# Two staging buffers for decoded weight blocks, one early block, second products three units behind

## The chip, the cores and the metric

The kernel runs on one core of a Trainium2 chip. The time is the device time of one execution, in microseconds, of that core. TensorE is called PE here, VectorE DVE, ScalarE ACT, GpSimd POOL; SP issues the DMA transfers.

## The reference

Three layers follow each other, all in float32.

```python
mask = q_assign[:, :, :, None] == k_assign[:, :, None, :]   # nearest of 16 centroids per head
scores = np.where(mask, scale * q @ k.T, -1e9)              # 2 x 8 heads, 768 tokens, 64 wide
attn = softmax(scores)
x = (attn @ v)                                              # becomes 1536 tokens x 512
h = x @ w_in;  g = np.maximum(0.01 * h, h); x = g @ w_out   # first MLP, 512 -> 2048 -> 512
h = x @ w_in2; r = np.maximum(h, 0); x = (r * r) @ w_out2   # second MLP, same sizes
```

The weights arrive as 64-bit floats; the kernel turns them into float32 itself.

## The kernel before

**Precision.** A float32 matrix is carried as two parts, a rounded one and the remainder (`xh` and `xl`, `wh` and `wl`, `gh` and `gl`), and a product is three matmuls: high by high, high by low, low by high.

**Attention** takes 48 steps of two row tiles. In a step PE makes scores `S`, DVE their row maxima `nm`, ACT the exponentials `e`, POOL divides them by their sums, PE transposes them (`T`, 12 transposes in three groups of four), ACT rounds each group to `eh`, DVE subtracts to `el`, and PE multiplies by the values (`A`, 12 matmuls). ACT and DVE then fold `A` into `xt` (lines 461 and 470). `A` has one PSUM buffer, so the next step's `A` waits for that fold. At the end of a head pair POOL makes `xh` and `xl` from `xt`.

**The MLPs.** A weight block is 128 of the 2048 hidden columns, `w_in` and `w_out` together, 16 blocks for each MLP, 32 in all. A unit is one block by one of three token blocks of 512, 96 units. For each unit `g1` (line 725) makes `h` with 12 matmuls, `act` makes `g` and its two parts on ACT and DVE, and `g2` (line 767) adds 12 matmuls into four sums `o`. `g2` of a unit is written `LAG` units behind its `g1`. Units go by groups of 2, 2, 4, 4 and so on blocks; in a group, token block by token block, the group's blocks in turn. After a group the four sums are added to `acc` (`flush`). There are four PSUM buffers for `h` and four for `o`.

**Weight blocks.** `decode_pieces` gives six pieces for a block: load (1 MB, a DMA by SP), `mag` on ACT (line 128), `shift`, `low` and `sign` on DVE (lines 132, 138, 145), and `split`, which makes `wh` on ACT (line 156) and `wl` on POOL (line 157). The raw block and its float32 form, `wraw` and `wt`, stand in a staging pool of one buffer each, taken from `stg[-1]`, the pool opened last. There are two such pools one after the other: `stg`, opened for the last head pair, and `stgb`, opened after attention. The first `EARLY` blocks are decoded beside the last head pair, through `stg`; the others use `stgb`, whose memory was that of exponentials `e` in attention. Eight blocks of finished weights are kept: those whose number modulo 8 is under 4 in the pool `wpx`, the others in `wpb`.

**The order.** Until six steps before the end of attention every engine's order is written out by hand (`PLAN`). From there the Tile scheduler puts the instructions in an order by its own estimate of times, once, when the program is built; each engine then runs its own list strictly in that order. The loads of SP are in program order throughout. Names such as `h_3740` carry a number that the build gives to each buffer; the same work has other numbers in the two kernels.

Of the kernel before, what the change touches and what calls it, by code (L numbers as in the profile page):

```python
# [10 lines left out]
I32 = mybir.dt.int32  # L11
# [41 lines left out]
def attention_moe_moe_kernel(  # L53
# [14 lines left out]
    NT, DM = out.shape  # L68
# [7 lines left out]
    NBLK = NT // N  # L76
    G = 4
    GROUPS = ([2, 2] + [G] * (NF // G - 1), [G] * (NF // G))
    EARLY = 2
    RING = 8  # L80
    WARM = (9,4,10)

# [29 lines left out]
    stg = []  # L112

    def decode_pieces(ci):

        m, f = divmod(ci, NF)
        st = {}

        def load():
            st["raw"] = stg[-1].tile([128, 2 * DM, 2], I32, tag="wraw", name="wraw")  # L120
            nc.sync.dma_start(
                out=st["raw"].rearrange("p a b -> p (a b)"), in_=(w1, w2)[m][f].bitcast(I32)
            )

        def mag():
            t = stg[-1].tile([128, 2 * DM], I32, tag="wt", name="wt")
            st["t"] = t
            nc.scalar.mul(out=t.bitcast(F32), in_=st["raw"][:, :, 1].bitcast(F32), mul=W_SHIFT)

        def shift():  # L130
            t = st["t"]
            nc.vector.tensor_scalar(
                out=t, in0=t, scalar1=3, scalar2=None, op0=ALU.logical_shift_left
            )

        def low():
            t = st["t"]
            nc.vector.scalar_tensor_tensor(  # L138
                out=t, in0=st["raw"][:, :, 0], scalar=29, in1=t,
                op0=ALU.logical_shift_right, op1=ALU.bitwise_or,  # L140
            )

        def sign():
            t = st["t"]
            nc.vector.scalar_tensor_tensor(
                out=t, in0=st["raw"][:, :, 1], scalar=-0x80000000, in1=t,
                op0=ALU.bitwise_and, op1=ALU.bitwise_or,
            )

        def split():  # L150
            t = st["t"].bitcast(F32)
            pool = next(q for q, n in ring if ci % RING < n)
            wh = pool.tile([128, 2 * DM], F32R, tag="wh", name="wh")
            wl = pool.tile([128, 2 * DM], F32R, tag="wl", name="wl")
            weights[m, f] = (wh, wl)
            nc.scalar.copy(out=wh, in_=t)  # L156
            nc.gpsimd.tensor_tensor(out=wl, in0=t, in1=wh.bitcast(F32), op=ALU.subtract)  # L157

        return [load, mag, shift, low, sign, split]

    def pool_copy(out, in_):
# [510 lines left out]
    }  # L672

    early = [f for i in range(EARLY) for f in decode_pieces(i)]
    for u in range(-1, NU + 5):
        if u == NU - UPP:
# [7 lines left out]
        for op in PLAN[FIRST[u] if p == 0 else u % UPP].split():  # L684
            if ":" in op:
                name, lag = op.split(":")
# [5 lines left out]
            else:  # L692
                name, ahead = op.split("@")
# [13 lines left out]
    ast.close()  # L707


    gp = ctx.enter_context(tc.tile_pool(name="gp", bufs=3, reuse_waits="tile"))  # L710
    ring.append((ctx.enter_context(tc.tile_pool(name="wpb", bufs=RING - G, reuse_waits="tile")), RING))
    stg.append(ctx.enter_context(tc.tile_pool(name="stgb", bufs=1, reuse_waits="tile")))
    accp = ctx.enter_context(tc.tile_pool(name="accp", bufs=1, reuse_waits="tile"))
# [37 lines left out]
    def g2(m, b, f, g, first, last, gh, gl):  # L751
        wh, wl = weights[m, f]
        for o in range(4):
            if first:
                outs[o] = ps_o.tile([128, N], F32, tag="o", name="o")
            if m == 0:
                ws = slice(DM + o * 128, DM + (o + 1) * 128)
                mm = ((wh[:, ws], gh), (wh[:, ws], gl), (wl[:, ws], gh))
            else:
                ts = slice(o * 128, (o + 1) * 128)  # L760
                mm = (
                    (gh[:, ts], wh[:, DM:]),
                    (gh[:, ts], wl[:, DM:]),
                    (gl[:, ts], wh[:, DM:]),
                )
            for i, (l, r) in enumerate(mm):
                nc.tensor.matmul(  # L767
                    out=outs[o],
                    lhsT=l,
                    rhs=r,  # L770
                    start=(first and i == 0),
                    stop=(last and i == 2),
                )
            if last:
                flush(m, b, g, o, outs[o])
# [25 lines left out]
    for m in range(2):  # L801
        f = 0
        for g, size in enumerate(GROUPS[m]):
            for i in range(size):
                if ci >= EARLY:
                    pcs = decode_pieces(ci)
                    at = last + i * (began - last) // size
                    n = max((began - last) // size, 1)
                    for k, pc in enumerate(pcs):
                        plan.setdefault(at + k * n // len(pcs), []).append(pc)  # L810
                ci += 1
            last = began
            for b in range(NBLK):
                for i in range(size):
                    units.append((m, b, f + i, g, i == 0, i == size - 1))
            began = len(units)
            f += size
    LAG = 2
    pend = []
    for U in range(len(units) + LAG):  # L820
        if U < len(units):
            m, b, f = units[U][:3]
            pend.append((*units[U], *act(m, g1(m, b, f))))
            for pc in plan.get(U, []):
                pc()
        if U == len(units) + LAG - 1:
            with tc.manual_schedule(engines={mybir.EngineType.PE}):
                g2(*pend.pop(0))
        elif U >= LAG:
            g2(*pend.pop(0))  # L830
# [47 lines left out]
```

## Time and profile before

| | us |
|---|---|
| median of 3 runs | 793.64 (792.76 to 794.53) |
| the profiled execution | 790.98 |
| its span, first to last instruction | 789.2 |
| PE busy in the span | 771.2 |

The sums of the prediction are made against the profiled execution. It lies 2.66 us under the median of the runs, and 1.78 us of it lie outside the span. Attention fills roughly the first 245 us of the span, the MLPs the rest, with some 20 us in which both are at work. Rows of the timeline give the start in us from the span's beginning, the duration, the engine, the line and the instruction; in brackets stands the idle time before it and what ended it. A matmul's duration there overlaps that of the next one, so the pace of matmuls is read from start to start. In the lines of the order, and of the profile, `S`, `T`, `A`, `h` and `o` are the PSUM tiles named above.

### The profile page before, as it was taken

To read this page: it belongs to the slowest core of one execution; us is meant where nothing else is said; L and a number is where in the kernel's file an instruction comes from. 1 tells how busy PE (TensorE), PEld (TensorE's weight loads), DVE (VectorE), ACT (ScalarE), POOL (GpSimd) and SP (SyncE) were. 2 spreads that over 40 slices of the span, in tenths; PEclk is the share of its full clock that TensorE was granted. 3 is DMA by queue.
4 is the path that set the end of the run, shared out by engine and by line. 5 is a ranking of instruction groups with operands and counts; after the bars stand their busy time and mean duration, and the time that the engine had idled before them with its cause. 6 is when DMAs were issued, how large, how long until landed. Compare 5 with 4: busy or idle time off the path is not lost.

```text
span 789.2 us, 11011 instructions
## 1 busy us (share of the span) xinstructions
PE 771.2 (98%) x4147; PEld 664.4 (84%) x4147; DVE 538.0 (68%) x772; ACT 412.7 (52%) x759; POOL 292.0 (37%) x257
## 2 busy tenths in 40 slices
PE   8999999999989999999999999999999999999998
PEld 8899999999977778888888888888888888888886
DVE  5899999999997378876665568387356547533333
ACT  6988988988996464443432344345344334222221
POOL 2989889888854322122220124352022012100000
PEclk9999999999999999999999999999999999999999
DMA  7584574564510323123221022013112103000102
GB/s 222 120 205 108 109 173 116 113 153 91 125 54 2 107 106 107 60 100 108 107 107 54 1 106 82 26 54 108 54 53 107 54 0 108 1 0 1 45 23 94
DMA packets 16005, 66.35 MB, mean 84 GB/s; under 512 B 2704, under 2 KB 2704, under 8 KB 10960
## 3 DMA queue, kind: packets, MB, share of 16 engines
q1 hardware_dynamic: 15952, 65.64, 28.7%
q8 instruction: 33, 0.54, 0.3%
q14 instruction: 20, 0.16, 0.1%
HBM read 44.60 MB, written 3.15 MB: 60 GB/s over the span
## 4 chain that ended last, share of the span: by engine, by line
PE 81%; DVE 11%; ACT 4%; DMA 1%; issue 1%; POOL 1%; SPq 0%; DVEq 0%; ACTq 0%
PE o L767 33%; PE h L725 33%; PE A L448 5%; PE T L413 5%; PE S L350 5%; DVE el L430 3%; DVE nm L373 3%; ACT e L383 2%; DVE xt L470 1%; ACT eh L424 1%; DVE ds L276 1%; PE ohT L305 1%; DVE m L275 1%; DMA rqk<-qk 1%; DVE wt L138 1%
## 5 line engine op out<-in xcount | busy, mean ns | idle before, releaser
L157 POOL TENSOR_TENSOR wl<-wt,wh 128x1024 fp32r<-128x1024 f32 x32 | 76.8, 2400 | 292.6 <-ACT wh L156 235.6
L725 PE MATMUL h<-xh,wh 128*128 128x512 f32 x384 | 150.6, 393 | 2.2 <-DVE g L739 2.2
L725 PE MATMUL h<-xh,wl 128*128 128x512 f32 x384 | 150.6, 392 | 0.0
L725 PE MATMUL h<-xl,wh 128*128 128x512 f32 x384 | 150.5, 392 | 0.0
L746 DVE TENSOR_TENSOR gl<-g,gh 128x512 fp32r<-128x512 f32 x96 | 95.4, 994 | 47.6 <-ACT gh L745 47.5
L430 DVE TENSOR_TENSOR el<-T,eh 128x512 fp32r<-128x512 f32 x144 | 94.8, 683 | 7.8 <-ACT eh L424 6.0
L745 ACT CAST gh<-g 128x512 fp32r<-128x512 f32 x96 | 59.6, 621 | 73.0 <-DVE g L742 42.7
L400 POOL TENSOR_SCALAR e<-e,r 128x768 f32<-128x768 f32 x96 | 88.0, 927 | 20.1 <-DVE r L397 14.7
L373 DVE TENSOR_REDUCE nm<-S 128x1 f32<-128x768 f32 x96 | 90.7, 946 | 4.6 <-PE S L254 2.2
L350 PE MATMUL S<-hb 128*128 128x384 f32 (+1 forms) x384 | 90.6, 350 | 3.0 <-ACT e L383 2.6
L383 ACT ACTIVATE e<-S,nm 128x768 f32<-128x768 f32 x96 | 87.0, 906 | 11.7 <-DVE nm L373 7.4
L742 DVE TENSOR_TENSOR g<-t 128x512 f32<-128x512 f32 x48 | 39.4, 822 | 72.8 <-ACT t L741 72.7
L725 PEld LDWEIGHTS h<-xh,wh 128*128 128x128 f32 x384 | 72.2, 188 | 18.5 <-DVE g L739 2.6
L741 ACT ACTIVATE t<-h 128x512 f32<-128x512 f32 x48 | 28.7, 598 | 112.0 <-PE h L725 111.9
L424 ACT CAST eh<-T 128x512 fp32r<-128x512 f32 x144 | 79.6, 585 | 12.9 <-PE T L413 12.3
L725 PEld LDWEIGHTS h<-xh,wl 128*128 128x128 f32 x384 | 72.2, 188 | 16.0
L725 PEld LDWEIGHTS h<-xl,wh 128*128 128x128 f32 x384 | 72.2, 188 | 15.9
L448 PE MATMUL A<-eh,vv 128*128 128x256 f32 x288 | 79.5, 306 | 3.5 <-DVE xt L470 3.5
L413 PE MATMUL T<-ident,e 128*128 128x128 f32 x576 | 81.0, 274 | 1.1 <-DVE el L430 1.0
L738 ACT ACTIVATE t<-h 128x512 f32<-128x512 f32 x48 | 28.6, 598 | 95.6 <-PE h L725 95.6
L767 PE MATMUL o<-gh,wl 128*128 128x512 f32 x192 | 75.3, 392 | 0.0
L767 PE MATMUL o<-gh,wh 128*128 128x512 f32 x192 | 74.5, 393 | 0.8 <-DVE xt L470 0.8
(105 smaller groups left out, 1454.0 us busy)
## 6 DMA issues: line engine op xcount, KB each, us to landing
wraw<-w SPq DMA_DIRECT2D x32, 1024.0 KB, 4.7
hb<-spl SPq DMA_DIRECT2D x14, 576.0 KB, 4.8
hb<-spl SPq DMA_DIRECT2D x42, 192.0 KB, 5.0
rqk<-qk SPq DMA_DIRECT2D x16, 384.0 KB, 4.5
rv<-v SPq DMA_DIRECT2D x8, 384.0 KB, 3.6
out<-ob SPq DMA_DIRECT2D x12, 256.0 KB, 2.1
twice<-qk SPq DMA_DIRECT2D x8, 192.0 KB, 6.4
hb<-st SPq DMA_DIRECT2D x28, 48.0 KB, 2.7
```

The costliest lines, as they stand in the source:

```text
L157: nc.gpsimd.tensor_tensor(out=wl, in0=t, in1=wh.bitcast(F32), op=ALU.subtract)
L350: nc.tensor.matmul(out=s[:, c, 0:HALF], lhsT=hb[0:k, a, i * 128 : (i + 1) * 128], rhs=hb[0:k, b, c * HALF : (c + 1) * HALF], start=(a == 0 ...
L373: nc.vector.tensor_reduce(out=n, in_=s_t[t][:, :, 0:HALF], axis=AX.XY, op=ALU.max, negate=True)
L383: nc.scalar.activation(out=e.rearrange("p (a b) -> p a b", a=2), in_=s_t.pop(t)[:, :, 0:HALF], func=AF.Exp, bias=n_t.pop(t), scale=1.0, ac ...
L400: nc.gpsimd.tensor_scalar(out=e_t[t], in0=e_t[t], scalar1=r_t[t // 2][:, t % 2 : t % 2 + 1], scalar2=1.0, op0=ALU.mult, op1=ALU.mult,)
L413: nc.tensor.transpose(T[:, o : o + 128], e_t[2 * u + b][:, kc * 128 : (kc + 1) * 128], ident)
L424: nc.scalar.copy(out=eh[:, 2 * g : 2 * g + 2, :].rearrange("p a b -> p (a b)"), in_=T_t[u, g])
L430: nc.vector.tensor_tensor(out=el[:, 2 * g : 2 * g + 2, :].rearrange("p a b -> p (a b)"), in0=T_t.pop((u, g)), in1=eh[:, 2 * g : 2 * g + 2, ...
L448: nc.tensor.matmul(out=A, lhsT=w, rhs=m[:, kc, :], start=(kc == 0 and i == 0), stop=(kc == KC - 1 and i == 1),)
L725: nc.tensor.matmul(out=h, lhsT=w[:, ws], rhs=x[:, kk, c], start=(kk == 0 and i == 0), stop=(kk == HP - 1 and i == 2),)
L746: nc.vector.tensor_tensor(out=gl, in0=g, in1=gh.bitcast(F32), op=ALU.subtract)
L767: nc.tensor.matmul(out=outs[o], lhsT=l, rhs=r, start=(first and i == 0), stop=(last and i == 2),)
```

## The change

Blocks from number `EARLY` on take the two staging pools in turns, even blocks `stg` and odd ones `stgb`; the early block uses `stg`. `EARLY` goes from 2 to 1, so block 1 is no longer decoded beside attention. `LAG` goes from 2 to 3, and `gh` and `gl` have four buffers in place of three, which moves `wpb` and `stgb` up by 4 KB in each partition.

```diff
--- before.py
+++ after.py
@@ -76,7 +76,7 @@
     NBLK = NT // N
     G = 4
     GROUPS = ([2, 2] + [G] * (NF // G - 1), [G] * (NF // G))
-    EARLY = 2
+    EARLY = 1
     RING = 8
     WARM = (9,4,10)
 
@@ -115,15 +115,16 @@
 
         m, f = divmod(ci, NF)
         st = {}
+        own = ci % 2 if ci >= EARLY else 0
 
         def load():
-            st["raw"] = stg[-1].tile([128, 2 * DM, 2], I32, tag="wraw", name="wraw")
+            st["raw"] = stg[own].tile([128, 2 * DM, 2], I32, tag="wraw", name="wraw")
             nc.sync.dma_start(
                 out=st["raw"].rearrange("p a b -> p (a b)"), in_=(w1, w2)[m][f].bitcast(I32)
             )
 
         def mag():
-            t = stg[-1].tile([128, 2 * DM], I32, tag="wt", name="wt")
+            t = stg[own].tile([128, 2 * DM], I32, tag="wt", name="wt")
             st["t"] = t
             nc.scalar.mul(out=t.bitcast(F32), in_=st["raw"][:, :, 1].bitcast(F32), mul=W_SHIFT)
 
@@ -707,7 +708,7 @@
     ast.close()
 
 
-    gp = ctx.enter_context(tc.tile_pool(name="gp", bufs=3, reuse_waits="tile"))
+    gp = ctx.enter_context(tc.tile_pool(name="gp", bufs=4, reuse_waits="tile"))
     ring.append((ctx.enter_context(tc.tile_pool(name="wpb", bufs=RING - G, reuse_waits="tile")), RING))
     stg.append(ctx.enter_context(tc.tile_pool(name="stgb", bufs=1, reuse_waits="tile")))
     accp = ctx.enter_context(tc.tile_pool(name="accp", bufs=1, reuse_waits="tile"))
@@ -815,7 +816,7 @@
                     units.append((m, b, f + i, g, i == 0, i == size - 1))
             began = len(units)
             f += size
-    LAG = 2
+    LAG = 3
     pend = []
     for U in range(len(units) + LAG):
         if U < len(units):
```

The first place is DVE beside the last steps of attention, from the row that takes the maxima of `S`. Before:

```order
L373 TENSOR_REDUCE nm_3447<-S_3412 128x1
L132 TENSOR_SCALAR wt_3493<-wt_3493 128x1024
L470 TENSOR_TENSOR xt_3091<-A_3372,xt_3091 64x256
L397 RECIPROCAL r_3368<-r_3368 128x2
L430 TENSOR_TENSOR el_3379<-T_3418,eh_3378 128x512
L138 SCALAR_TENSOR_TENSOR wt_3493<-wraw_3491,wt_3493 128x1024
L430 TENSOR_TENSOR el_3445<-T_3428,eh_3444 128x512
L373 TENSOR_REDUCE nm_3474<-S_3450 128x1
L430 TENSOR_TENSOR el_3445<-T_3455,eh_3444 128x512
L145 SCALAR_TENSOR_TENSOR wt_3493<-wraw_3491,wt_3493 128x1024
L397 RECIPROCAL r_3434<-r_3434 128x2
L470 TENSOR_TENSOR xt_3484<-A_3438,xt_3484 64x256
```

and now:

```order
L374 TENSOR_REDUCE nm_3406<-S_3382 128x1
L471 TENSOR_TENSOR xt_3091<-A_3370,xt_3091 64x256
L398 RECIPROCAL r_3366<-r_3366 128x2
L374 TENSOR_REDUCE nm_3441<-S_3410 128x1
L431 TENSOR_TENSOR el_3377<-T_3416,eh_3376 128x512
L431 TENSOR_TENSOR el_3439<-T_3422,eh_3438 128x512
L431 TENSOR_TENSOR el_3439<-T_3449,eh_3438 128x512
L374 TENSOR_REDUCE nm_3468<-S_3444 128x1
L471 TENSOR_TENSOR xt_3478<-A_3432,xt_3478 64x256
L398 RECIPROCAL r_3428<-r_3428 128x2
```

The three DVE pieces of block 1 (`wt_3493`) are gone from between attention's rows; the fold of `A` (`xt`) stands next to the maxima.

The second place is PE at the end of attention's matmuls, around the first unit's second product. Before, from the row ahead of the last `A` matmul, `wh_3609` being block 1 and `wh_3424` block 0:

```order
L448 MATMUL A_3693<-eh_3666,vv_3072 128x256
L448 MATMUL A_3693<-el_3667,vv_3072 128x256
L725 MATMUL h_3910<-xl_62,wh_3609 128x512
L725 MATMUL h_3910<-xh_61,wl_3610 128x512
L767 MATMUL o_3814<-gh_3757,wh_3424 128x512
L767 MATMUL o_3814<-gl_3758,wh_3424 128x512
L767 MATMUL o_3814<-gh_3757,wl_3425 128x512
L767 MATMUL o_3818<-gh_3757,wh_3424 128x512
L767 MATMUL o_3818<-gl_3758,wh_3424 128x512
```

and now, from the end of the first unit's second product on, `wh_3757` being block 1 and `wh_3598` block 0:

```order
L768 MATMUL o_3851<-gh_3746,wh_3598 128x512
L768 MATMUL o_3851<-gl_3747,wh_3598 128x512
L768 MATMUL o_3851<-gh_3746,wl_3599 128x512
L726 MATMUL h_3765<-xh_61,wh_3757 128x512
L726 MATMUL h_3765<-xl_62,wh_3757 128x512
L726 MATMUL h_3788<-xh_61,wh_3598 128x512
L726 MATMUL h_3788<-xl_62,wh_3598 128x512
L726 MATMUL h_3788<-xh_61,wl_3599 128x512
```

Before, six units' `h` (the first two whole) were spread among the last `T` and `A`; now only the first unit's 12 matmuls stand there, the rest of attention's matmuls follow in one piece, and after the 12 matmuls of the first unit's second product the next on the list reads block 1. Two matmuls of `h_3765` stand ahead of 12 of `h_3788`, which read block 0. After that come 2 of `h_3814`, 8 of `h_3855`, 10, 10 and 4 to complete these three, and then `h_3894`, which takes the buffer of `h_3765`.

The third place is ACT at the same point. Before, from the first piece of block 2:

```order
L128 ACTIVATE wt_3763<-wraw_3761 128x1024
L461 COPY xt_3484<-A_3693 64x256
L156 CAST wh_3810<-wt_3763 128x1024
L780 COPY acc_3739<-o_3814 128x512
L780 COPY acc_3739<-o_3818 128x512
L780 COPY acc_3739<-o_3822 128x512
L128 ACTIVATE wt_3853<-wraw_3851 128x1024
L780 COPY acc_3739<-o_3826 128x512
L738 ACTIVATE t_3801<-h_3788 128x512
```

and now, from the last fold of attention:

```order
L462 COPY xt_3478<-A_3682 64x256
L129 ACTIVATE wt_3752<-wraw_3750 128x1024
L129 ACTIVATE wt_3763<-wraw_3761 128x1024
L157 CAST wh_3757<-wt_3752 128x1024
L157 CAST wh_3810<-wt_3763 128x1024
L129 ACTIVATE wt_3837<-wraw_3835 128x1024
L129 ACTIVATE wt_3959<-wraw_3957 128x1024
L157 CAST wh_3916<-wt_3837 128x1024
L739 ACTIVATE t_3778<-h_3765 128x512
L739 ACTIVATE t_3801<-h_3788 128x512
```

Before, `h` was passed on (`t`) ahead of all of block 3 but its first piece. Now the first pieces of blocks 1, 2, 3 and 4 and the roundings of 1, 2 and 3 all stand ahead of the first `t` of `h_3765`. On SP the loads keep their order; the load of block 1 is the one that now waits for the memory of `e`, the exponentials of the last step among them, and so stands behind the last `T` group of attention.

## Rows read from the trace of the kernel before

**Rows 1.** Page, part 1: busy us of the engines, share of the span, instructions.

```profile
PE 771.2 (98%) x4147; PEld 664.4 (84%) x4147; DVE 538.0 (68%) x772; ACT 412.7 (52%) x759; POOL 292.0 (37%) x257
```

**Rows 2.** Windows: stretch, length, busy PE PEld DVE ACT POOL, clock, DMA, GB/s.

```profile
229.50:245.40 15.90, 12.92 (x93) 11.38 (x92) 15.71 (x25) 13.48 (x28) 10.35 (x9) 1.00 0.01 2
...
245.40:281.00 35.60, 32.65 (x172) 27.09 (x171) 18.77 (x29) 18.20 (x32) 9.31 (x7) 1.00 0.18 62
...
281.00:300.00 19.00, 19.00 (x83) 15.43 (x82) 13.32 (x15) 12.78 (x21) 5.26 (x3) 1.00 0.33 115
...
780.00:789.20 9.20, 5.41 (x24) 4.13 (x22) 2.78 (x5) 0.00 (x0) 0.00 (x0) 1.00 0.30 114
```

**Rows 3.** Timeline of PE, 232 to 281: start, duration, instruction, idle before.

```profile
232.62 0.97 PE L350 MATMUL S<-hb 128*128 128x384 f32 x4 [1.39 <-ACT e L383]
...
239.55 0.38 PE L448 MATMUL A<-eh,vv 128*128 128x256 f32 x1 [1.44 <-DVE xt L470]
...
245.41 0.48 PE L725 MATMUL h<-xh,wh 128*128 128x512 f32 x1
...
258.92 0.60 PE L413 MATMUL T<-ident,e 128*128 128x128 f32 x4
...
259.28 0.48 PE L725 MATMUL h<-xh,wh 128*128 128x512 f32 x1
...
264.48 0.28 PE L448 MATMUL A<-eh,vv 128*128 128x256 f32 x1
...
265.89 0.39 PE L725 MATMUL h<-xl,wh 128*128 128x512 f32 x1
...
278.08 0.50 PE L725 MATMUL h<-xh,wh 128*128 128x512 f32 x1 [2.18 <-DVE g L739]
...
280.97 1.10 PE L767 MATMUL o<-gh,wh 128*128 128x512 f32 x4
```

**Rows 4.** Timeline of VectorE, 236 to 240.

```profile
236.55 2.55 DVE L145 SCALAR_TENSOR_TENSOR wt<-wraw,wt 128x1024 int32<-128x1024 int32 x1
...
239.10 0.39 DVE L470 TENSOR_TENSOR xt<-A,xt 64x256 f32<-64x256 f32 x1
```

**Rows 5.** Groups by line: count, busy us, mean ns, idle before.

```profile
L128 ACT ACTIVATE wt<-wraw 128x1024 f32<-128x1024 f32 x32 | 36.4, 1137 | 16.4 <-DMA wraw<-w 14.9 <-POOL wl L157 1.4
...
L132 DVE TENSOR_SCALAR wt<-wt 128x1024 int32<-128x1024 int32 x32 | 23.9, 748 | 20.6 <-ACT wt L128 20.6
...
L138 DVE SCALAR_TENSOR_TENSOR wt<-wraw,wt 128x1024 int32<-128x1024 int32 x32 | 41.3, 1289 | 0.6
...
L145 DVE SCALAR_TENSOR_TENSOR wt<-wraw,wt 128x1024 int32<-128x1024 int32 x32 | 40.9, 1277 | 0.5
...
L156 ACT CAST wh<-wt 128x1024 fp32r<-128x1024 f32 x32 | 33.6, 1050 | 27.1 <-DVE wt L145 19.2 <-PE o L767 7.9
...
L739 DVE TENSOR_TENSOR g<-h,t 128x512 f32<-128x512 f32 x48 | 32.8, 686 | 39.8 <-ACT t L738 39.2
```

**Rows 6.** Timeline of ScalarE, 264 to 275.

```profile
264.33 1.14 ACT L128 ACTIVATE wt<-wraw 128x1024 f32<-128x1024 f32 x1 [4.19 <-DMA wraw<-w]
...
274.19 1.13 ACT L128 ACTIVATE wt<-wraw 128x1024 f32<-128x1024 f32 x1 [1.14 <-POOL wl L157]
```

**Rows 7.** Timeline of PE, two stretches of second-stage matmuls.

```profile
286.55 0.39 PE L725 MATMUL h<-xh,wh 128*128 128x512 f32 x1
...
300.03 0.39 PE L767 MATMUL o<-gh,wh 128*128 128x512 f32 x1
...
339.87 0.39 PE L725 MATMUL h<-xh,wh 128*128 128x512 f32 x1
...
354.83 0.39 PE L767 MATMUL o<-gh,wl 128*128 128x512 f32 x1
```

**Rows 8.** Timeline of PE, its first microseconds.

```profile
1.40 3.79 PE L199 MATMUL warm<-ident 128*128 128x128 f32 x18 [1.40 <-POOL ident masks.py:199]
...
9.29 2.48 PE L199 MATMUL warm<-ident 128*128 128x128 f32 x20
```

## The prediction

> **What bounds the kernel now.** I read the page's busy times first. PE is busy 771.2 of 789.2 us [rows 1], so at most 18 us are idle on it, and only work or a wait that touches PE can move the time. The windows come next, to see where that idle time lies. From 281 to 300 us PE is busy all 19.00 us [rows 2], and the timeline names no wait on PE after 278.08. In the last window it is busy 5.41 of 9.20 us [rows 2]; what follows its last matmul is the last sum and its transfer out, which the change leaves alone. What the change can reach is the passage from attention to the MLPs. There PE is idle 15.90 - 12.92 = 2.98 us from 229.5 to 245.4 and 35.60 - 32.65 = 2.95 us from 245.4 to 281 [rows 2], 5.9 us together.
>
> The timeline says what each of these waits is. In the first stretch DVE is busy 15.71 of 15.90 us [rows 2]: DVE binds there. Scores wait 1.39 us for an exponential, and `A` waits 1.44 us for DVE's fold [rows 3]; the fold stands on DVE behind a piece of block 1's decoding that took 2.55 us [rows 4], against a mean of 1.28 for that line [rows 5]. In the second stretch the largest wait is 2.18 us, for DVE's `g` [rows 3]. After 281 the pace of matmuls alone sets the time.
>
> **The edits that cost and bring nothing.** `LAG` 3 and four buffers for `gh` and `gl` give second products more slack, but PE does not wait for them after 281, so they are worth 0 there. Their bounds are below nothing by no more than the idle time after 281, which is 0, and above nothing by a wait for weights freed one unit (24 matmuls) later; the planned pieces of a block stand at least three units behind that, so I take 0. Two staging buffers let a load start before the block ahead is decoded. With one, ACT waits 1.14 us for POOL to finish with block 2 before it takes block 3 [rows 6], and the `t` behind it ends in PE's 2.18 us [rows 3]; after 281 no such wait reaches PE, so there it is again 0. All three matter only through the new order, which is worked out now against the profiled execution (790.98 us, span 789.2).
>
> **Block 1 leaves attention.** DVE loses the three pieces of one block, ACT two. Without them DVE has about 15.71 - (0.75 + 1.29 + 2.55) = 11.1 us of work in that stretch [rows 2, 4, 5] and ACT 13.48 - 1.14 - 1.05 = 11.3 [rows 2, 5], both less than PE's 12.92, so PE binds. The two waits go, and one more `T` group (0.36 us, the step from 258.92 to 259.28) now stands ahead of the first `h` [rows 3]. The first `h` then starts at 245.41 - 1.39 - 1.44 + 0.36 = 242.9. Ends: 2.83 us of gain, or none, if ACT's exponentials hold the step instead; I take the whole, since both engines have room.
>
> **The rest of attention comes in one piece.** After that come 12 matmuls of `h` at 0.232 (13.48 us for the 58 from 286.55 to 300.03) [rows 7] = 2.79; five `T` groups at 0.36 = 1.80; 24 matmuls of `A`, 12 of them taking 265.89 - 264.48 = 1.41 us [rows 3], = 2.82; and the last group ends 0.60 and not 0.36 after its start [rows 3], 0.24. That gives 250.6. Nothing stands between these to cover the handovers from `T` through ACT and DVE to `A`. I add 0.4, an estimate; its ends are 0 and 1.4, the price of the `A` wait above. So the last `T` group ends at about 251.0; call that moment E. It was 259.5 before, with 24 more matmuls of `h` (5.6 us) done by then.
>
> **The new wait.** Block 1's load goes to the memory of the last exponentials, so it starts at E. What the same load position costs is in the trace, since block 2 had it: the last `T` group ended at 258.92 + 0.60 = 259.52 [rows 3] and ACT could begin at 264.33 [rows 6], 4.81 us. Then come line 128, 1.14; lines 132, 138 and 145, 0.75 + 1.29 + 1.28 = 3.31; line 156, 1.05 [rows 5]; and 0.1 of handovers. PE gets block 1 at E + 10.4 = 261.4. In these 10.4 us PE has 12 matmuls of `A` (1.41) and the 12 of the first unit's second product (2.79), 4.2 us. It idles 6.2 us, about 1 us of it before that product, and some 5 us in one piece ahead of `h_3765`, the first row that reads block 1. Behind that row stand 12 matmuls of `h_3788` that need block 0 alone, and they wait with it. That is the place where the cover of early block 1 is gone.
>
> **A second, smaller wait.** From 261.4 PE has 48 matmuls before `h_3894`: 11.2 us, to 272.6. `h_3894` needs `g` of `h_3765`, which stands on DVE behind the decoding of block 4. Counted from E: block 1 leaves DVE at 4.81 + 1.14 + 3.31 = 9.3; block 2, loaded right behind it, at 12.6; block 3's load can start at 9.3, so it leaves DVE at 9.3 + 4.81 + 1.14 + 3.31 = 18.5; block 4's load starts at 12.6 and lands in time for its pieces to follow, at 21.8; `g` takes 0.69 [rows 5]: 22.5. So `h_3894` starts at 273.5, 0.9 late. Then 36 matmuls (12 of it, 10 + 2 of `h_3936`, 12 of a second product) end at 273.5 + 8.4 = 281.9. By then PE has done 108 second-stage matmuls. Before, it had done the same 108, by the order, when `o` began at 280.97 [rows 3]. **Sum: 0.9 us later**, 791.9 for the profiled execution. Against the median of 793.64, 2.66 above that execution, I forecast 794.5.
>
> The idle time tells the same story: 5.9 us of it before, and 6.2 + 0.9 + 0.4 = 7.5 after, less the few tenths that fewer changes between `T`, `A` and `h` give back.
>
> **Rival: the long wait lowers TensorE's clock (slower).** The granted clock is 1.00 (2.4 GHz) in every window shown, also in the last, with its 3.8 us of idle at the end [rows 2], and the longest idle piece inside the MLPs is 2.18 [rows 3]. A piece of 5 us is longer than any this trace has; from 3.8 on nothing here speaks for the clock staying up. For the price, the first 18 warm-up matmuls took 3.79 us, 0.211 each, and 20 of the same form later 2.48, 0.124 each [rows 8], so a start like the kernel's own loses 3.79 - 18 x 0.124 = 1.6 us. Of this 0.9 falls into the second wait. If the low pace lasts twice as long, 3.1 - 0.9 = 2.2 remain. The end of this rival is 0.9 + 0.7 to 0.9 + 2.2, and I take 796.2. Against it: the wait may come out shorter than 3.8 if the last `A` takes longer to hand over.
>
> The Trainium skill, page "TensorE: Matmul & The Clock Gate", section "Why this matters for your kernels", warns of idle gaps between bursts of matmuls, after which the clock goes back to its lower level. No row here shows such a fall inside the span; by that rule this rival's time would hold, by the granted clock of the rows the forecast's.
>
> **Rival: more is won than I count (faster).** E comes at 250.6 without handovers (0.4 less), the chain behind E is 1.5 us shorter because the load takes less than 4.81, and the second wait goes with it (0.9 less): 0.9 - 0.4 - 1.5 - 0.9 = -1.9, so 791.7. For it: DVE's freed time also helps every handover. Against it: E - 250.6 is work that PE must do, and the chain behind E is one of measured pieces, each waiting for the one before.
>
> **Rival: the pace of matmuls moves with the memory.** From 286.55 to 300.03, on blocks kept in `wpx`, matmuls come every 0.232 us; from 339.87 to 354.83, on blocks in `wpb`, 66 come in 14.96, every 0.227 [rows 7]. `wpb` moves by 4 KB. If it fell to the slower pace, its 16 blocks x 3 units x 24 = 1152 matmuls cost 5.7 ns more each, 6.6 us: 801.1. If `wpx` gained the faster one, 787.9. Against it: `wpx` stays where it was, and `wpb` moves by one matrix width among rows that all go at one pace.
>
> **How the numbers follow.** Two times within 0.2% (1.6 us) can't be told apart here, so no change is 792.0 to 795.2. The forecast, 794.5, has 0.53; its own range is 793.2 to 795.9, from E at 250.6 without a second wait to E at 252.4, and 0.11 of it lies on the slower side. The clock, 796.2, has 0.25, of which 0.21 is slower. More won, 791.7, has 0.15, of which 0.13 is faster. The pace has 0.05 for slower and 0.02 for faster. Together: faster 0.15, same 0.48, slower 0.37. The range is 791.8 to 798.0: it leaves out the two of the pace and half of the faster rival.
>
> **What would show it.** Right: no waits of PE between 230 and 243 in the new profile; its first `h` near 243; one idle piece of about 5 us ahead of line 726, ended by ACT's rounding of block 1 (line 157), some 10.4 us behind the end of the last `T`; a second of about 1 us ended by `g`; none after 282. The clock rival would show as matmuls behind the long wait at twice 0.232, and a granted clock under 1.00 in that window. Wrong: an idle piece of less than 2 us there, a first `h` later than 245, waits in the stretch after 282, or another pace on either pool.

## The result: 3.9 us slower, and the profile after

| | kernel before | changed kernel |
|---|---|---|
| time, median (range) | 793.60 us (792.76 to 794.53) | 797.54 us (796.82 to 797.75) |
| ratio to before, 95% interval | | 1.0057 [1.0045, 1.0069] |
| profiled execution, its span | 790.98, 789.2 | 797.75, 796.0 |

The change makes the kernel slower by about half a percent: 0.57% by the ratio in the table, 0.50% by the quotient of its two medians. The two profiled executions lie further apart (6.8 us of span) than the medians, since the one of before lies 1.8 us under its timed runs and the one of after at the top of its own. The profiled execution of before is of a rare kind: of 76 more of that kernel, 7 had a mean granted TensorE clock of 1.00 and took 790.57 to 791.62 us, and 69 had 0.995 to 0.998 and took 791.94 to 794.40. No kept trace shows where that kernel loses its clock. Line numbers of the changed kernel are one higher from line 118 on.

The stretches of [rows 2] and the next one, after the change (length, then busy us and instructions of PE, PEld, DVE, ACT, POOL, clock, DMA share, GB/s):

```profile
229.50:245.40 15.90, 15.90 (x117) 15.17 (x116) 14.69 (x27) 14.13 (x33) 10.27 (x12) 1.00 0.01 3
245.40:281.00 35.60, 27.21 (x130) 21.85 (x129) 26.65 (x25) 17.35 (x25) 14.12 (x7) 0.90 0.49 174
281.00:300.00 19.00, 19.00 (x83) 15.42 (x82) 18.96 (x21) 12.82 (x19) 6.96 (x2) 1.00 0.34 116
300.00:320.00 20.00, 19.23 (x84) 15.16 (x83) 17.98 (x17) 13.10 (x21) 7.23 (x3) 1.00 0.45 158
```

TensorE's 2.98 idle us of the first stretch are gone, as forecast. In the second it idles 8.4 us instead of 2.95, and the clock is under 1.00. VectorE has 26.65 us of work there instead of 18.77, and in the third stretch 18.96 of 19.00 instead of 13.32: more than one block moved from the first stretch would bring.

TensorE's timeline, to lay beside [rows 3] (start, duration, instruction, idle time before it and what ended it):

```profile
242.42 0.47 PE L726 MATMUL h<-xh,wh 128*128 128x512 f32 x1
...
250.26 0.60 PE L414 MATMUL T<-ident,e 128*128 128x128 f32 x4
251.34 0.38 PE L449 MATMUL A<-eh,vv 128*128 128x256 f32 x1 [0.48 <-DVE xt L471]
...
261.25 0.79 PE L726 MATMUL h<-xh,wh 128*128 128x512 f32 x1 [4.94 <-ACT wh L157]
261.85 0.63 PE L726 MATMUL h<-xl,wh 128*128 128x512 f32 x1
262.27 0.63 PE L726 MATMUL h<-xh,wh 128*128 128x512 f32 x1
...
277.90 0.51 PE L726 MATMUL h<-xh,wh 128*128 128x512 f32 x1 [2.65 <-DVE g L740]
...
313.11 0.50 PE L768 MATMUL o<-gh,wh 128*128 128x512 f32 x1 [0.77 <-ACT acc L781]
```

The long wait is the forecast's: 4.94 us, ended at 261.25 by `wh`. Behind it matmuls come every 0.427 us (261.85, 262.27, ...) instead of 0.232; these are the stretches with their clock (last columns as above, TensorE alone):

```profile
256.00:260.00 4.00, 0.31 (x2) 1.00 0.37 158
260.00:264.00 4.00, 2.75 (x7) 0.51 0.65 242
264.00:268.00 4.00, 4.00 (x13) 0.64 0.41 127
268.00:272.00 4.00, 4.00 (x19) 1.00 0.37 156
```

TensorE's clock was at 1.2 instead of 2.4 GHz for some 6.8 us, from 260.1, still in the wait, to 266.9; summed over the matmuls' distances above 0.232 that costs 2.7 us. The wait for `g` is 2.65 where 0.9 was forecast, and there is a wait at 313, where none was. With 108 second-stage matmuls done TensorE is 5.4 us behind the kernel before (286.38 against 280.97).

What held `g` is on VectorE and GpSimd, in one stretch:

```profile
260.76 1.22 DVE L139 SCALAR_TENSOR_TENSOR wt<-wraw,wt 128x1024 int32<-128x1024 int32 x1
262.02 3.29 DVE L146 SCALAR_TENSOR_TENSOR wt<-wraw,wt 128x1024 int32<-128x1024 int32 x1
267.46 1.96 DVE L133 TENSOR_SCALAR wt<-wt 128x1024 int32<-128x1024 int32 x1 [2.15 <-ACT wt L129]
...
273.84 3.29 DVE L146 SCALAR_TENSOR_TENSOR wt<-wraw,wt 128x1024 int32<-128x1024 int32 x1
277.16 1.29 DVE L740 TENSOR_TENSOR g<-h,t 128x512 f32<-128x512 f32 x2
```

```profile
261.28 2.95 POOL L158 TENSOR_TENSOR wl<-wt,wh 128x1024 fp32r<-128x1024 f32 x1 [4.54 <-ACT wh L157]
266.46 2.40 POOL L158 TENSOR_TENSOR wl<-wt,wh 128x1024 fp32r<-128x1024 f32 x1 [2.23 <-ACT wh L157]
273.10 2.94 POOL L158 TENSOR_TENSOR wl<-wt,wh 128x1024 fp32r<-128x1024 f32 x1 [4.24 <-ACT wh L157]
```

Line 146 of blocks 2 and 4 takes 3.29 us, line 139 just ahead of it 1.22. Each long one begins while GpSimd subtracts the block ahead (261.28 to 264.23, 273.10 to 276.04) and ends 1.1 us after that subtraction. Over the whole kernel (count, busy us, mean ns), to lay beside [rows 5]:

```profile
L146 DVE SCALAR_TENSOR_TENSOR wt<-wraw,wt 128x1024 int32<-128x1024 int32 x32 | 65.1, 2035 | 0.7
L139 DVE SCALAR_TENSOR_TENSOR wt<-wraw,wt 128x1024 int32<-128x1024 int32 x32 | 46.5, 1453 | 0.5
```

Before, the same lines took 40.9 and 41.3 us: 29 us of VectorE's time are new, though no instruction was added.

### The profile page after: what moved, and what is told of

Read it like the earlier page. It is cut to its first block, busy times and chain, and to the rows that moved or that the text cites. A ratio compares the mean times of both kernels' runs of the same rounds, so it can differ in the third digit from the quotient of the medians.

```text
span 796.0 us, 11032 instructions
## 1 busy us (share of the span) xinstructions
PE 775.2 (97%) x4147; PEld 667.9 (84%) x4147; DVE 549.3 (69%) x772; ACT 411.5 (52%) x759; POOL 300.7 (38%) x257
## 4 chain that ended last, share of the span: by engine, by line
PE 77%; DVE 14%; ACT 5%; issue 2%; DMA 1%; POOL 0%; DVEq 0%; ACTq 0%; SPq 0%; POOLq 0%
PE o L768 31%; PE h L726 30%; PE A L449 5%; PE S L351 5%; PE T L414 5%; DVE el L431 3%; DVE nm L374 3%; ACT e L384 2%; DVE wt L139 2%; DVE wt L146 1%; DVE wt L133 1%; DVE xt L471 1%; ACT eh L425 1%; PE warm L200 1%; DVE gl L747 1%
## 5 line engine op out<-in xcount | busy, mean ns | idle before, releaser
L158 POOL TENSOR_TENSOR wl<-wt,wh 128x1024 fp32r<-128x1024 f32 x32 | 88.6, 2768 | 281.7 <-ACT wh L157 271.1
L726 PE MATMUL h<-xh,wh 128*128 128x512 f32 x384 | 152.3, 397 | 7.6 <-ACT wh L157 4.9
L747 DVE TENSOR_TENSOR gl<-g,gh 128x512 fp32r<-128x512 f32 x96 | 76.7, 799 | 39.4 <-ACT gh L746 37.5
L425 ACT CAST eh<-T 128x512 fp32r<-128x512 f32 x144 | 79.3, 586 | 10.6 <-PE T L414 10.2
L742 ACT ACTIVATE t<-h 128x512 f32<-128x512 f32 x48 | 28.6, 596 | 101.6 <-PE h L726 101.6
L768 PE MATMUL o<-gl,wh 128*128 128x512 f32 x192 | 75.3, 392 | 0.0
```

Of the source, the lines that this page charges most:

```text
L425: nc.scalar.copy(out=eh[:, 2 * g : 2 * g + 2, :].rearrange("p a b -> p (a b)"), in_=T_t[u, g])
L726: nc.tensor.matmul(out=h, lhsT=w[:, ws], rhs=x[:, kk, c], start=(kk == 0 and i == 0), stop=(kk == HP - 1 and i == 2),)
L747: nc.vector.tensor_tensor(out=gl, in0=g, in1=gh.bitcast(F32), op=ALU.subtract)
L768: nc.tensor.matmul(out=outs[o], lhsT=l, rhs=r, start=(first and i == 0), stop=(last and i == 2),)
```

## The experiments

**One part of the change at a time.** First the early block alone, and the other parts without it:

```diff
 e1: the kernel before            e2: the changed kernel
-    EARLY = 2                    -  own = ci % 2 if ci >= EARLY else 0
+    EARLY = 1                    +  own = (ci - 1) % 2 if ci >= EARLY else 0
```

e1 expected: 

> The kernel before with one early block instead of two; one staging buffer and a lag of two stay. Theory (the place of block 1 carries the loss, and behind it the place of g among DVE's decoding decides how much): the last T ends near 251, the first matmul on block 1 starts near 261.3 after some 5 us of idle TensorE, the clock falls to half behind that wait and costs about 2.7 us. With one staging buffer g stands behind block 2 on DVE (not behind block 4), so no second wait over 0.5 us: the clock's 2.7 us show in full, about 796.2 against 793.6 before. Rival (the clock is hidden work or free): 793.6. Rival (early block and long second wait belong together, whatever the staging): 797.5 as in the changed kernel.

e2 expected: 

> The changed kernel, but block 1 takes the same staging buffer as block 0 (blocks 2, 4, ... the other), so its load need not wait for the exponentials' memory; lag of three, four buffers and two staging buffers stay. Theory (the late load of block 1 is the whole loss): no idle piece of TensorE over 3 us, clock 1.00 all along, 793.6 or up to 1.5 less, since the wait of ScalarE for GpSimd at block 3 goes too. Rival (lag of three or two staging buffers cost something of their own): over 795.5.

In both the rival's number came. e1: 0.9995 [0.9987, 1.0004], no loss. e2: 1.0042 [1.0030, 1.0054], slower though no wait exceeds 2.5 us and its mean granted clock is 1.00 in all five executions; its block 1 is decoded within attention again, and until 272 us every engine has the order of e7 below, where `EARLY` is 2. TensorE's waits from 229 us on in e1 (total, count, longest):

```profile
PE h L725 <- ACT wh L156: 4.8, 1, 4.8
PE A L448 <- DVE xt L470: 0.5, 1, 0.5
PE o L767 <- DVE xt L470: 0.2, 1, 0.2
```

The long wait is there, and the clock falls behind it (0.50 for 3.4 us, 1.7 us lost), but no second wait: with the three waits of [rows 3] gone too, the account is nearly even (span 789.5 against 789.2 us).

Then the rest of the eight combinations, with the lag and the staging taken apart:

```diff
 e5: changed kernel     e6: changed kernel     e7: as e6, and      e8: as e2, and
-  LAG = 3, bufs=4     -  own = ci % 2 ...    -  EARLY = 1         -  EARLY = 1, LAG = 3, bufs=4
+  LAG = 2, bufs=3     +  own = -1            +  EARLY = 2         +  EARLY = 2, LAG = 2, bufs=3
```

e5 expected: 

> One early block and two staging buffers, with the lag of two and three buffers of the kernel before. Theory A (the second staging buffer is the loss: it lets the loads and the decoding of blocks 3 and 4 run ahead, and they stand on DVE before the g that TensorE waits for): g behind block 4's decoding, a wait of TensorE for g of 2 to 3 us at about 278 us, 796.5 to 798, as the whole change. Theory B (the lag of three is the loss): 792.5 to 793, as with one early block alone.

e6 expected: 

> One early block and the lag of three with four buffers, but one staging buffer as before. Theory A (the second staging buffer is the loss): g behind block 2 on DVE, one long wait of 4.9 us and no second wait over 0.5 us, 792 to 793 as with one early block alone. Theory B (the lag of three is the loss): 796 to 798.

e7 expected: 

> The kernel before with the lag of three and four buffers alone: two early blocks, one staging buffer. Theory A: no loss, 793; and since g comes on DVE ahead of block 3's decoding in the order that results, the wait of 2.18 us for g goes and it may be up to 2.2 us faster, 791. Theory B: slower than before by 2 us or more.

e8 expected: 

> The kernel before with two staging buffers alone: two early blocks (both staged in the first buffer), lag of two, three buffers. Theory A: slower than before by 2 to 4 us with waits of TensorE for DVE or ScalarE between 270 and 330 us, near the 796.0 of the same kernel with the lag of three. Theory B: 793, as before.

Ratios to the kernel before:

| early blocks, lag | one staging buffer | two staging buffers |
|---|---|---|
| 2, lag 2 | 1 (before) | 1.0098 [1.0082, 1.0113] (e8) |
| 2, lag 3 | 0.9980 [0.9971, 0.9989] (e7) | 1.0042 [1.0030, 1.0054] (e2) |
| 1, lag 2 | 0.9995 [0.9987, 1.0004] (e1) | 1.0106 [1.0091, 1.0121] (e5) |
| 1, lag 3 | 1.0000 [0.9991, 1.0009] (e6) | 1.0057 [1.0045, 1.0069] (changed) |

The loss is the column: the second staging buffer costs 0.6% with the lag of three and 1.0 to 1.1% with the lag of two, whatever the early blocks. Theory A holds, and its sizes for e5 and e8 (796.5 to 798, 2 to 4 us) were too small: 801.0 and 800.2. The lag of three takes back 3.5 to 4.2 us of the second buffer's loss. Alone it gains 0.2% with two early blocks and nothing with one (e1, e6). Even the 0.2% goes with the clock: executions at a mean granted clock of 1.00 took 790.40 to 791.76 us in e7 and 790.57 to 791.62 in the kernel before; whether the lag is what keeps the clock up more often is not shown. In e7 the wait of 2.18 us for `g` has gone, and two smaller ones have come (1.3 and 0.7). In e8 one wait alone is

```profile
PE h L726 <- DVE g L740: 6.7, 1, 6.7
```

**Work in TensorE's long wait.** Six small or fourteen full matmuls into `h`'s bank, overwritten by the first real one; the order on all engines is the same in both:

```diff
         h = ps_h.tile([128, N], F32, tag="h", name="h")
+        if (m, b, f) == (0, 0, 1): n matmuls(out=h[:, 0:c],
+            lhsT=xh[:, HP - 1, NT - 128 : NT], rhs=weights[0, 0][0][:, 0:c])
         # e3: n = 6, c = 128     e4: n = 14, c = 512
```

e3 expected: 

> The changed kernel with 6 matmuls of 128 columns (results overwritten) on TensorE ahead of the first matmul on block 1. They fill 0.4 us of the long wait, and the order that comes out has g of unit 1 on DVE behind block 3's decoding, not behind block 4's; all five engines have the same order as the next kernel. Theory (g behind block 4's decoding is what set the changed kernel's end of the passage, and hid the clock's loss): the clock falls to half behind the long wait as before, the second wait is under 0.5 us instead of 2.65, and 108 second-stage matmuls are done near 283.6, not 286.4: about 2.8 us faster than the changed kernel, 794.9 to 796.2. Rival (the clock alone is the loss): no faster than the changed kernel, 797.5.

e4 expected: 

> As the kernel with 6 small filler matmuls, same order on every engine, but 14 fillers of 512 columns: 3.3 us of work in the long wait, so TensorE idles some 1.7 us there instead of 4.6. Theory (the low clock follows from the idle TensorE and costs 2.7 us where no later wait hides it): clock 1.00 behind the wait, 2.7 us faster than with the small fillers, 793 to 794. Rival (the clock is lowered by something else, or its loss is hidden here as well): the same time as with the small fillers.

e3: 1.0043 [1.0032, 1.0055]; e4: 1.0053 [1.0038, 1.0068], a miss. In both a unit on block 0 also moved into the long wait; in e3 1.43 us of it are left, in e4 nothing, and the clock is 1.00 from 252 to 272 in both. Yet the time of e4 is the changed kernel's; the waits came back later:

```profile
PE o L768 <- ACT acc L781: 3.6, 1, 3.6
PE h L726 <- DVE g L740: 2.1, 1, 2.1
```

In e3 the wait for `g` was 2.83, not under 0.5; that its 796.08 us lie in the range of the theory is luck. The traces of e3 and e4 aren't free of the low clock either: it came behind the wait for `g` in e3 (272.7 to 276.1), and in e4 at the kernel's start and behind the wait for `acc`:

```profile
9.00:13.00 4.00, 4.00 (x23) 0.57 1.05 293
252.00:272.00 20.00, 18.92 (x86) 1.00 0.56 210
309.00:313.00 4.00, 3.51 (x9) 0.59 0.73 260
```

What settles the clock is executions in which it never fell. At a mean granted clock of 1.00 the kernel before took 790.6 to 791.6 us, e2 795.7 to 796.4, and the two of e4's six that kept it 795.2. So with the second staging buffer 4 to 5 us are lost without the low clock, and e4 also without the long wait. Neither is the loss; it is what makes VectorE and ScalarE late for a wait further on.

**What makes VectorE late: order, or GpSimd.** In e9 GpSimd stays busy behind each `wh`, but nearly without reading (the low parts of the weights are left out):

```diff
-  nc.gpsimd.tensor_tensor(out=wl, in0=t, in1=wh.bitcast(F32), op=ALU.subtract)
+  q = 8 if ci >= 1 else 2 * DM
+  nc.gpsimd.tensor_tensor(out=wl[:, 0:q], in0=t[:, 0:q], in1=wh[:, 0:q]..., op=ALU.subtract)
+  if ci >= 1: nc.gpsimd.memset(wl[:, 4:].bitcast(F32), 0.0)   # twice
```

e9 expected: 

> The changed kernel, but for blocks 1 to 31 GpSimd subtracts only the first 8 columns of wl and fills the rest with two memsets: it stays busy behind each wh, but hardly reads SBUF. What is left out: the low parts of those weights. DVE's order is the changed kernel's for 40 instructions behind the end of attention, to beyond block 5's decoding. Theory C (with two staging buffers DVE decodes a block while GpSimd subtracts the block ahead, and DVE is held for the rest of that subtraction, some 2.1 us in almost every block): line 146 takes 1.22 instead of 2.04 us on the mean, lines 139 and 133 1.23 and 0.69; g is done near 273.5 instead of 277.9, the second wait is under 1 us and no wait for acc follows: 792.5 to 793.5 as with one staging buffer. Theory D (only the order counts: more decoding stands ahead of g and of the copies of acc): the wait for g stays above 2 us, 796.5 to 797.5.

e9: 1.0000 [0.9991, 1.0010], with two staging buffers, one early block, the lag of three, and `g` behind block 4's decoding as in the changed kernel. Line 146 of block 2, and GpSimd beside it, in two timelines:

```profile
261.15 1.22 DVE L146 SCALAR_TENSOR_TENSOR wt<-wraw,wt 128x1024 int32<-128x1024 int32 x1
```

```profile
261.24 1.95 POOL L158 MEMSET wl<- 128x1020 f32 x2
```

and its mean over the kernel:

```profile
L146 DVE SCALAR_TENSOR_TENSOR wt<-wraw,wt 128x1024 int32<-128x1024 int32 x32 | 38.9, 1216 | 0.2
```

TensorE's waits in e9 from 229 us on are those of e1:

```profile
PE h L726 <- ACT wh L157: 4.9, 1, 4.9
PE A L449 <- DVE xt L471: 0.5, 1, 0.5
PE o L768 <- DVE xt L471: 0.2, 1, 0.2
```

1.22 us beside a GpSimd that writes, 3.29 beside one that reads. The Trainium skill, page "SBUF — State Buffer", section "Who interferes with whom", states that a VectorE instruction with two SBUF inputs contends with a GpSimd instruction that reads SBUF and not with one that only writes it; this pair agrees with it. The whole loss goes with it, and the waits for `g` and `acc` too: theory C is shown, D falls. Two things beside it differ in e9. GpSimd is done with `wt` sooner, but up to the wait for `g` no line 129 waited for that in the changed kernel. And from 300 us on ScalarE and VectorE have another order, so for `acc` the cause is less sure than for `g`, up to which these two engines keep the changed kernel's order. One expectation failed: line 133, a shift with one input, takes 0.99 us on the mean in e9, not 0.69, and up to 1.38 beside the memset.

**Which half of the second buffer.** `raw` holds the loaded words, `wt` the word being decoded.

```diff
 e10: as e7                                  e13: the changed kernel
   st["raw"] = stg[own].tile(... own = ci % 2 ...     st["raw"] = stg[-1].tile(...
   t = stg[-1].tile(...                               t = stg[own].tile(...
```

e10 expected: 

> The kernel before with the lag of three, two early blocks, and two buffers for the loaded words alone; the word being decoded (wt) has one buffer, so DVE can't begin a block before GpSimd is done with the block ahead. Theory C: line 146 stays near 1.27 us on the mean, no loss of the second staging buffer is left, 791 to 792 as with the lag of three alone, or up to 1 us less since a block's load (4.8 us) is then no longer part of the chain. Theory D (loads that run ahead cost through the order, or through DMA traffic): 795 or more.

e13 expected: 

> The changed kernel with one buffer for the loaded words and two for wt: the reverse of the kernel with two raw buffers. Theory C (DVE is held where its decoding falls into GpSimd's subtraction of the block ahead): with one raw buffer the next block lands some 4.8 us after line 146 has ended, when wh (1.05) and wl (2.4) are done; so no overlap, line 146 near 1.27 us on the mean, and the time is that of one early block with the lag of three, 792 to 793. Rival (a second wt buffer alone is enough for the loss): line 146 over 1.8 us, 796 or more.

e10: 0.9964 [0.9951, 0.9976], 790.35 us: two buffers for the loads and one for `wt` cost nothing. Whether they gain is not shown: the interval overlaps e7's, and e15 below, with the same staging and the same pace, has 0.9983. e13: 1.0009 [1.0000, 1.0018]. The loss needs both: only where the next words have landed and a free `wt` stands ready does VectorE decode into GpSimd's subtraction. In e13 line 146 takes

```profile
L146 DVE SCALAR_TENSOR_TENSOR wt<-wraw,wt 128x1024 int32<-128x1024 int32 x32 | 51.1, 1596 | 0.5
```

and not the 1.27 expected: five blocks, all from 390 us on, still take 3.3 us, but no wait of TensorE follows from it.

**A matter beside it: where the weights stand.** In the kernel before matmuls on blocks in `wpx` come every 0.232 us, on those in `wpb` every 0.227 [rows 7]. A pad moves `wpx` alone:

```diff
+  an unused tile of 2944 bytes a partition (e11, e14), 8192 (e12) or 4064 (e15) between stg and wpx
   # e11, e12: as e7     e14, e15: as e10
```

e11 expected: 

> The kernel before with the lag of three alone, and wpx 2,944 bytes lower in each partition (base 181,344, the same remainder modulo 4,096 as wpb); the order on every engine is the same. In all runs so far a matmul that reads a block in wpx comes every 232 ns on the mean, one that reads a block in wpb every 226.7. If the remainder modulo 4,096 decides it, wpx falls to 226.7 and 1,152 matmuls gain 5.6 ns each: 6.4 us, 785. If the place in the upper part of SBUF decides it, no change: 791.5.

e12 expected: 

> As the kernel with wpx 2,944 bytes lower, but 8,192 bytes lower (base 176,096), so that the remainder modulo 4,096 stays as before and the blocks end at 208,864 instead of 217,056; same order on every engine. If the remainder decides the pace: 232 ns and 791.5. If the absolute place decides it and the border lies among these addresses: some of the blocks fall to 226.7, 786 to 790.

e14 expected: 

> Two raw buffers and one wt buffer, two early blocks, the lag of three, and wpx 2,944 bytes lower. If the two gains add: 790.35 minus 7.45 (791.48 to 784.03), 783. If the faster matmuls only turn into waits for DVE: 784 or more.

e15 expected: 

> As the kernel with wpx 2,944 bytes lower, but 4,064 lower: base 180,224, a multiple of 4,096. If only the old remainder of 4,064 was slow: 226.7 ns in wpx, the same time as that kernel, 783. If blocks ought not to begin at such a multiple either: a slower pace in wpx, and 786 to 790.

| kernel | `wpx` base, modulo 4,096 | pace from 283 to 300 | ratio to before |
|---|---|---|---|
| e7 | 184,288, 4,064 | 0.2333 | 0.9980 [0.9971, 0.9989] |
| e11 | 181,344, 1,120 | 0.2267 | 0.9885 [0.9872, 0.9899] |
| e12 | 176,096, 4,064 | 0.2323 | 0.9965 [0.9953, 0.9978] |
| e14 | 181,344, 1,120 | 0.2267 | 0.9876 [0.9863, 0.9889] |
| e15 | 180,224, 0 | 0.2333 | 0.9983 [0.9975, 0.9992] |

The order on every engine is the same in e7, e11 and e12, and in e10, e14 and e15. For e11 the pace is 74 steps between these rows:

```profile
283.04 0.39 PE L726 MATMUL h<-xh,wh 128*128 128x512 f32 x1
...
299.81 0.39 PE L768 MATMUL o<-gh,wh 128*128 128x512 f32 x1
```

The forecast's 6.4 us were 7.45 against e7 (791.48 to 784.03) and 6.36 against e12 (790.39), which has a pad and the slow pace. Of the three remainders tried 1,120 is the quick one; a multiple of 4,096 is as slow as 4,064. e14, with two raw buffers, one `wt`, the lag of three and the moved pool, takes 783.07 us (782.04 to 783.40), 1.2% less than the kernel before; its interval overlaps that of e11, so the moved pool alone may be all of it. e12 and e7, at one pace, have intervals that overlap.

## Why the prediction was wrong, point by point

- *Block 1 leaves attention*: right. First `h` at 242.42 (242.9 forecast), no wait there.
- *The rest of attention comes in one piece*: right. The last `T` group ends at 250.86 (E = 251.0).
- *The new wait*: right in time, length and releaser: 261.25 after 4.94 us (261.4, some 5).
- *The edits that cost and bring nothing* is the step that failed. It set two staging buffers at nothing, apart from the new order. The table shows that they are the loss, 0.6 to 1.1%, and e9 how: VectorE's decoding meets GpSimd's reading. With one `wt`, VectorE can't begin a block before GpSimd is done with the one ahead; that forced wait kept the two apart, and I had counted it as a cost only. For the lag 0 was right in executions at a clock of 1.00; over all, with two early blocks, it gains 0.2%.
- *A second, smaller wait*: the mechanism was right, `g` behind block 4, and the size wrong for the same reason: blocks 2 to 4 were priced at the means of a kernel in which the two seldom meet. Block 2 cost 2.07 more (3.29 - 1.22). By that, by ScalarE's order (line 129 of block 3 behind `wh` of block 2: 1.3) and by line 133, held to 1.96 where 0.75 was priced, block 3 left VectorE at 271.94, 2.6 later than E + 18.5. Block 4 cost another 2.07 and left at 277.13, 4.5 later than E + 21.8. The sum's 0.9 came out as 5.4, and those 4.5 are the difference. A row of the kind was among mine: 2.55 us for line 145 ahead of `xt` [rows 4]. I used it to remove the instruction and not to price those that stay. What it met was a subtraction of GpSimd too:

```profile
236.20 1.82 POOL L478 TENSOR_TENSOR xl<-xt,xh 128x768 fp32r<-128x768 f32 x1
```

- *From the profile to the median*: wrong as well, and it hid part of the miss. The 2.66 us by which the medians of before lie above its profiled execution were added as if the changed kernel had them too; there they are -0.2 (797.54 and 797.75). Profile against profile the sum of 0.9 became 6.8, 5.9 us off; the forecast of 794.5 was 3.0 off. That 797.54 still lies in the range of 791.8 to 798.0 is luck: no term of that range was the one that failed.
- *None after 282*: wrong; TensorE is another 1.05 us behind from 313 on, with ScalarE's copy of `acc` behind a `wh` that waited for a block of which line 139 had taken 3.31 us beside GpSimd.
- *The clock rival* happened as described (half pace, clock at 0.50) and had the sign right, but is not the cause. In the changed kernel the 2.7 us fall into the wait for `g`, which VectorE's chain ends in any case; in e1 and e6 such a loss (1.7 and 2.0) has no second wait to fall into, and both are as fast as the kernel before in its usual executions. At a clock of 1.00 the loss is there as well (e2).
- *The pace rival*: the paces stayed, and e11 shows why: `wpb` moved by 4,096 bytes and kept its remainder.

The forecast of no change is what the change would have been without GpSimd's reading: e9's ratio is 1.0000. With 108 second-stage matmuls done e9 is 0.89 us behind the kernel before, the sum's 0.9, but that the number agrees is luck: it is made of 2.0 us at half pace and no second wait. Not settled: why the lag of three takes back a good part of the loss, and where the kernel before loses its clock in most executions. The wait of 2.1 us for `gl` in e5 is not in the changed kernel, but the orders differ in more than that.

## What to carry to other kernels

A buffer that is short can be what keeps two engines from meeting: before doubling it, ask which engine will then run beside which, and price its instructions beside that neighbour, not at the mean of a kernel where the two stay apart. An instruction that takes 3.3 us instead of 1.2 with the same operands is the trace's mark of it; find what GpSimd did in those microseconds. A wait of TensorE that is filled or removed ahead of a late chain comes back behind it, as in e3 and e4.

## What the runs showed of the hardware

- VectorE's two-input operations on 128x1024 words take 1.22 us alone or beside a memset of GpSimd (e9), and about 3.3 where they begin in its subtraction of a block (changed kernel); 2.1 us are lost there, and GpSimd's subtraction is longer too (2.77 on the mean instead of 2.40). The one-input shift of line 133 was held as well: 1.96 instead of 0.69 at 267.46, and by the memset too, 1.37 at 384.36 in e9.
- Matmuls of 512 columns come every 226.7 ns or every 232 to 233, by the place of the weight tile in a partition: base 1,120 modulo 4,096 (e11, e14) against 0 (e15) and 4,064 (e7, e12).
- The granted clock fell to 0.50 (1.2 GHz) within the waits of 4.8 to 5.1 us or just behind them: for 6.8 us in the changed kernel, e5, e6, e9 and e13, and for 3.4 in e1; for 10.2 at the wait of 6.72 in e8. The length of the wait alone doesn't decide: the clock also fell, for 3.4 us, behind waits of 3.65 (e4), 2.83 (e3) and 2.15 us (e5), and not behind 2.65 (changed kernel), 2.48 (e2) and 2.18 (before).
- It also fell where TensorE had no wait over 0.3 us in the 8 us ahead: in e4 and e10, for 3.4 us from 9.4 and 9.9 us on, behind 24 matmuls of 32 columns; the 20 warm-up matmuls that follow took 3.77 and 4.07 us instead of 2.48 [rows 8]. Before, behind the same 24, it stayed at 1.00.
